# A gated recurrence and a mixer on one core: part of the transposes moved from TensorE to the DMA crossbar

## The chip, the cores and the metric

The kernel runs on one core of one Trainium2 chip. The metric is the device time of one launch in microseconds. PE is TensorE, DVE is VectorE, ACT is ScalarE, POOL is GpSimd, and SP is the sync engine, which here issues most of the DMAs.

## The reference

Two parts follow each other. The first is linear attention with a decaying state, for 4 batches, 8 heads, 768 steps and 48 channels a head:

```python
state = alpha[:, :, t, :, None] * state + np.einsum('bhd,bhe->bhde', k[:, :, t], v[:, :, t])
y[:, :, t] = np.einsum('bhd,bhde->bhe', q[:, :, t], state)
```

The second is a mixer on x, which is y with its heads side by side (4 x 768 x 384):

```python
xt = x.transpose(0, 2, 1)
h = np.maximum(xt @ w_tok1, 0.0) @ w_tok2        # 768 -> 256 -> 768, over the steps
u = x + h.transpose(0, 2, 1)
h2 = np.maximum(u @ w_ch1, 0.0) @ w_ch2          # 384 -> 1536 -> 384, over the channels
return u + h2
```

Inputs and output are float32; the kernel multiplies in bfloat16.

## The kernel before, in words

**Attention.** The 768 steps of a batch are six chunks of 128, numbered 0 to 23 over the four batches. For chunks 6 to 23 (`attention`, one chunk at a time) ACT takes the logarithm of alpha (line 412), PE sums it over the steps with a triangular matrix (lines 418 and 421), and ACT takes two exponentials, `a` and `ia` (lines 426 and 428). POOL makes `pkk`, k times `ia` (line 434); POOL or DVE makes `pkq`, q times `a` (line 438). Both have the steps on the partitions. The scores need them with the channels there, so PE transposes them in eight blocks into one bank of PSUM (line 454, operations `trk` and `trq`), and ACT or DVE copies the bank to SBUF as `tp` (line 458). Sixteen small matmuls make the scores (line 469), DVE masks them (line 472), and PE adds the scores times v (line 507) and q times the state before (line 511) to the chunk's output, which is copied out as `x` (line 515). The state goes on from chunk to chunk without the transposed tiles (lines 483, 492 and 498). Batch 0 has a version for pairs of chunks (`attention_pair`).

**Mixer.** For each batch PE runs the two token layers (lines 766 and 788), DVE adds x to give `u` (line 798, six tiles of 128 steps), PE transposes u in two halves of nine blocks (line 834, `utp`; the first half of batch 0 is made in another way), and ACT or DVE copies them as `ut` (line 840). The first channel layer (line 853, 72 matmuls a batch) is followed by a rectifier on ACT or DVE (lines 860 and 861), the second channel layer (line 875) by an addition of u on DVE (line 881), and the output leaves through SP (line 884).

**Loads.** k, q, v and alpha of batches 1 to 3 are loaded by SP, one chunk of one tensor at a time (192 KB in rows of 192 bytes, line 733), into a few buffers each; those of batch 0 in pairs of chunks (line 744); the weights and batch 0's v by POOL.

**What sets the order.** A planner in Python runs at build time: every operation has a cost, its inputs and a rank (`RANKS`, a list of names; the lowest rank goes first), and `schedule` runs them through a model of engines, buffers and DMA queue. The instructions are then written out in the order that the model gave, so each engine, SP's queue too, has a fixed order, and it waits where an input is late. In the model a DMA from SP starts 1.0 us after its issue or when the one before it is through, takes its given time, and has landed 1.2 us later:

```python
t = max(issue + 1.0, self.hw_end)
...
self.hw_end = t + left
return t + left + 1.2
```

`LOADS` ranks the loads of batch 0, `NOT_BEFORE` holds some DMAs back, and warm-up matmuls without a use fill the gaps on PE up to about 36 us (line 377).

Of the kernel before, what the change touches and what calls it, by code (L numbers as in the profile page):

```python
# [9 lines left out]
BF16 = mybir.dt.bfloat16  # L10
# [34 lines left out]
utp3_1_1 ch1_3_0_10 rt1_0_7 ch1_0_0_5 gt4 ch2_0_5_1 y17 ss14 ch1_2_0_5 rt2_1_3 trq20 u1_1 ch2_3_2_1 trq12 ea21
tok1_1_0_5 tok2_0_4 ea23 tk5 vb23 ch1_2_1_11 ch1_3_0_7 u3_0 u3_2 ch2_3_1_1 u0_2 ss12 ei8 kk3 st12 mask5 ht2_1 aq11
kk17 trk18 aq5 mask14 ln15 tp9 ht0_0 ch2_2_2_1 sa20 ln7 gt22 ch1_3_1_9 tok2_1_0 tok1_1_1_3 ln12 o2_2 rt3_0_11 tk0
ss1b ei9 st16 rt0_1_5 u2_5 u0_1 y2 o3_5b qq4 rt3_0_6 ch2_2_3_1 o2_1 ei18 trk4 aq0 trk21 ut0_0_1 ss2 tp7 ln19 ln5 y1
cum7 cum2 y0 gt16 ea4 tok1_0_1_5 y21 vb12 ln2 ea19 o3_4 ea8 rt1_0_5 ch1_3_0_6 ch1_0_0_0 ei5 ch1_2_0_10 st15 rt0_0_3
rt2_1_7 aq7 vb19 out3_0 rt3_0_2 ut1_1_1 sa7 ut3_1_0 rt3_1_5 out2_4 ei7 tok2_3_4 mask10 ei13 tt0_1 trk9 ei2 ln21  # L50
ch2_2_2_2 mask7 trq23 utp1_0_0 ch1_1_1_10 rt0_1_10 ei23 ea11 ch1_3_1_7 ch1_1_1_5 o3_3 lvz2 cum15 out3_2 rt1_1_10
ch1_0_1_7 sa22 st21 out1_5 trk8 ss7 ch2_3_2_0 ch1_0_0_1 kk6 qq5 tp18 x7 ss3 gt15 cum8 tp16 trq22 kk0 aq23 ss1 qq23
ln4 wwt1 u1_0 st18 st20 x10 utp0_1_0 qq14 ch2_1_2_0 ch1_3_0_0 out0_3 rt0_1_7 aq10 rt3_1_2 rt2_1_1 o3_5a trk23 ln18
x3 ut2_1_1 rt0_1_3 out3_3 trk20 gt0 st3 st7 rt3_1_9 st1 rt2_1_2 tp6 tok2_0_3 ch1_0_0_2 ut2_1_0 trk16 wwc20 rt1_1_4
ea10 rt3_0_9 ch1_0_0_3 st4 y9 tok2_0_5 rt1_1_11 wwc10 y16 trq3 ch1_0_0_11 utp0_1_1 rt3_0_1 ln1 ss6 ch1_3_1_6
ch1_3_1_2 ea3 ch1_0_0_9 rt0_1_0 trq19 trq8 ch1_1_1_0 tok1_3_0_0 u3_3 x17 aq15 tok2_0_2 qq10 x1 qq21 tok2_3_0 out3_1
ch2_1_0_2 lvz5 trq13 aq16 ch1_0_1_4 tok2_0_1 ch1_0_1_1 ch1_0_1_11 aq12 rt1_0_1 cum11 ch1_0_1_6 trq11 out1_4 tok2_3_1
tok1_3_0_3 ch1_0_0_7 ch1_2_0_7 ch1_0_1_3 o2_3 ut0_0_0 vb22 tok2_1_1 tok2_0_0 mask15 ea12 trq21 st14 u2_0 gt3
ch2_0_2_1 tok2_1_3 wwc21 ch1_0_1_5 aq3 u0_4 rt0_0_11 st22 ch1_0_1_0 vb16 trk7 tp23 wwc22 mask8 ss3b rt0_0_8 trq5
qq19 rt2_1_10 ch1_0_1_9 mask21 ss5 rt0_1_4 ei1 tok1_1_0_0 ln22 tok2_2_1 ch2_3_4_2 rt3_0_10 tk1 tok1_1_1_5 ln9 st19  # L60
out0_4 utp1_0_1 y7 ch1_0_1_10 rt0_0_6 ch2_3_5a_1 kk15 x15 kk8 rt3_0_4 ch1_0_1_8 ch2_0_0_0 aq18 utp2_0_1 rt1_0_11
out3_4 out1_1 ch2_2_4_0 ch2_3_0_0 y11 ch2_0_5_0 ea15 ch1_3_1_5 vb13 o0_4 tq3 u2_1 rt3_1_4 aq1 ch1_3_1_1 rt2_1_6
tok1_3_1_0 qq20 ch2_0_1_0 ss4 ch2_2_0_2 ch2_0_3_0 tok2_1_5 tp10 ss22 trq0 ch1_1_1_9 ch1_3_0_8 mask4 y23 u0_0
ch1_3_0_5 rt0_0_9 tok1_0_1_3 o1_2 vb21 mask6 rt0_1_9 tok1_0_0_5 ch1_2_1_2 rt2_1_0 tok2_1_4 rt3_0_8 st5 lvz0 mask3
utp3_0_1 rt1_0_9 cum22 aq8 kk13 ch2_2_1_1 ss21 ch2_3_1_0 rt1_0_2 trq10 out1_3 ln3 kk19 gt14 rt3_0_3 rt2_0_3 tok2_2_2
ch2_3_1_2 mask13 ch1_2_1_1 ut2_0_1 ch1_1_1_7 kk22 ch1_2_0_4 ln8 tq1 tok1_3_1_5 o2_4 aq17 o3_1 ch2_2_5_2 ht1_1 ei12
aq20 y22 ss15 y18 ln14 ch1_2_1_7 kk5 ch1_1_1_2 ss10 gt11 rt1_0_6 st3b ch1_2_0_2 ch2_1_3_2 st13 rt0_1_6 ss16
ch2_0_3_2 y12 rt1_1_2 out0_5 ch1_1_0_10 tq5 cum0 u2_2 tok1_2_0_5 vb20 out3_5b x22 tok2_2_0 rt2_1_5 ht1_0 ch2_3_0_1
vb6 out0_0 cum20 ch1_1_0_5 vb7 gt17 x4 rt3_1_0 ei4 rt2_0_5 o2_5 gt10 utp2_1_0 ch1_1_1_6 aq13 ei20 cum6 ch1_3_1_0
rt0_0_4 ch2_1_1_1 trk22 o0_0 ch2_3_4_1 ea7 wwc12 ch1_1_1_8 ch1_1_0_1 rt0_0_0 trk14 ei21 ln20 ch2_0_1_2 cum18 u1_2  # L70
ch1_2_1_8 ch1_2_0_3 ch1_1_0_2 ss19 ch2_1_1_0 rt2_0_7 rt3_1_6 out1_2 o3_0 out2_5 ch2_2_1_2 ch1_2_1_3 tok2_2_4 u2_3
ch1_3_0_3 qq0 tq0 rt0_1_1 cum19 rt1_0_0 ei17 ch2_3_5b_2 u0_3 x2 ln11 ch1_2_1_10 o0_5 x12 wwc11 trq18 ht3_1 rt0_0_10
qq9 rt2_0_11 ch2_3_2_2 ch1_1_0_0 vb14 ch1_1_0_3 o2_0 tok1_2_1_3 y5 st8 ei10 ss2b tp21 qq15 rt2_0_9 aq6 trk11 y15
ei22 tok1_2_1_5 aq14 ch1_2_0_8 rt0_0_2 utp2_1_1 sa14 ch2_1_2_2 trq14 ch1_3_1_3 ch1_1_0_9 x19 tok1_2_0_0 rt3_1_8 kk11
rt0_1_2 mask18 trk15 utp1_1_0 vb8 tp22 o0_1 kk1 u0_5 mask9 trk0 ch1_1_0_6 rt3_1_7 ch1_3_1_8 ch1_1_0_11 ch1_2_0_1
ch1_2_0_0 ch2_2_0_1 qq16 ss18 rt2_1_8 u3_5 ch1_3_0_1 out2_2 ut1_0_0 ea0 x13 cum14 sa21 aq2 ea9 rt0_0_7 ea5 st0
ch1_2_1_5 sa16 ch2_3_5a_2 ch2_1_5_2 st1b ch1_1_0_4 kk7 y19 out2_1 mask22 ch2_1_3_0 ln6 tp14 x14 st2b tok2_2_5 cum13
ln16 o1_5 o1_1 trq4 ei15 out3_5a y20 ch2_1_5_0 ch1_3_1_11 ch2_2_3_0 o0_2 ch1_1_0_8 ch2_2_4_1 mask20 ch2_2_5_0 aq4
ea1 ch2_2_0_0 ch2_3_4_0 ch2_1_4_0 x20 trk2 aq22 tp19 ht0_1 trk13 lvz3 ch2_0_4_1 tp12 cum10 tok2_3_2 rt2_0_0 x11 trk5
rt2_0_4 u1_3 ch1_3_0_9 ch2_1_4_2 utp1_1_1 ut3_0_0 ut3_1_1 ch2_2_2_0 y14 trq16 vb10 ln10 gt18 mask1 ch2_1_0_0 qq6  # L80
# [129 lines left out]
def schedule(ops, slots, sw=()):  # L210
# [20 lines left out]
    while ready:  # L231
# [41 lines left out]
        if o.dma:  # L273
            o.done = dmas.land(o.dma[0], t, *o.dma[1:])
# [779 lines left out]
```

## Time and profile before

| | us |
|---|---|
| median of 3 runs | 184.79 |
| lowest and highest run | 184.6 and 186.39 |
| the profiled execution, its own time | 182.94 |
| span of the profiled execution, first to last instruction | 181.2 |
| PE, DVE, ACT, POOL busy in it | 173.9, 105.4, 108.5, 59.7 |

The profile is that of one execution. The busy times are of the whole span and mix stages: loads are on the way up to about 117 us, and only outputs after it. PE busy counts a matmul from its start to a modelled end, so it is read together with the pace of uninterrupted runs. A row of the groups gives the line, the engine, the tiles out and in, the count, the busy time, the mean of one in nanoseconds, and the idle time ahead with what ended it. A row by stretches gives the busy time of PE, weight loads, DVE, ACT and POOL with counts, then the granted clock, the busy share of the DMA engines and what they moved in GB/s.

### The profile page before, as it was taken

How to read it: one execution, taken by the hardware profiler on the slowest of the kernel's cores; microseconds unless marked ns; L12 is line 12 of the kernel's file. 1: busy time of each engine (PE TensorE's matmuls, PEld its weight loads, DVE VectorE, ACT ScalarE, POOL GpSimd, SP SyncE). 2: the span in 40 equal slices, each digit the busy share in tenths (PEclk: the TensorE clock that was granted, in tenths of full speed). 3: DMA queues.
4: the chain of work that ended last, by engine and by line, in shares of the span. 5: the costliest groups of instructions: out<-in, count | busy, mean ns of one | idle time of the engine just before them, and what ended most of it. 6: DMA issues, size and time to landing. Idle time of an engine off the chain costs nothing.

```text
span 181.2 us, 4740 instructions
## 1 busy us (share of the span) xinstructions
PE 173.9 (96%) x1922; PEld 120.7 (67%) x1922; DVE 105.4 (58%) x190; ACT 108.5 (60%) x219; POOL 59.7 (33%) x94
## 2 busy tenths in 40 slices
PE   7897899999999999999899999999999999999994
PEld 4575788677676676677677666577666566676663
DVE  6674676694972665886975579565556652130142
ACT  3456785577894567799787675879732204948000
POOL 8922886020942336456361722403030000000000
PEclk9999999999999999999999999999999999999999
DMA  5999999998999899999999999910002121110123
GB/s 133 201 202 245 225 176 200 194 191 171 203 196 198 159 194 178 201 185 238 205 217 182 228 169 205 259 60 4 0 0 89 45 87 43 47 43 0 43 90 130
DMA packets 93861, 26.45 MB, mean 146 GB/s; under 512 B 88080, under 2 KB 93456, under 8 KB 93840
## 3 DMA queue, kind: packets, MB, share of 16 engines
q1 hardware_dynamic: 87984, 22.42, 59.6%
q0 software_dynamic: 5856, 3.74, 14.2%
q8 instruction: 15, 0.25, 0.6%
q14 instruction: 6, 0.05, 0.1%
HBM read 25.17 MB, written 4.72 MB: 165 GB/s over the span
## 4 chain that ended last, share of the span: by engine, by line
PE 64%; DMA 23%; SPq 4%; ACT 2%; DVE 2%; issue 1%; POOL 1%; DVEq 0%; POOLq 0%; ACTq 0%
PE ps L853 21%; PE ps L875 19%; DMA at_pair<-in_alpha_dram 15%; SPq L744 4%; PE ps L766 3%; PE ps L788 3%; DMA vt_pair<-in_v_dram 3%; PE ps L454 3%; DMA qt_pair<-in_q_dram 3%; DMA at<-in_alpha_dram 3%; PE ps L377 2%; PE p L469 2%; PE ps L834 1%; PE ps L507 1%; PE ps L666 1%
## 5 line engine op out<-in xcount | busy, mean ns | idle before, releaser
L853 PE MATMUL ps<-ut,wc 128*128 128x384 bf16 x288 | 54.3, 326 | 0.9 <-DVE ut L840 0.5
L875 PE MATMUL ps<-wc,rt 128*128 128x384 bf16 (+1 forms) x300 | 52.7, 319 | 0.0
L860 ACT ACTIVATE rt<-ps 128x384 bf16<-128x384 f32 x85 | 41.8, 494 | 12.9 <-PE ps L853 12.4
L853 PEld LDWEIGHTS <-wc 128*128 128x128 bf16 x288 | 30.7, 114 | 13.3 <-issue 1.7
L875 PEld LDWEIGHTS <-rt 128*128 128x128 bf16 x300 | 27.8, 98 | 15.5
L881 DVE TENSOR_TENSOR o<-ps,u 128x384 f32<-128x384 f32 (+1 forms) x25 | 13.3, 540 | 21.6 <-PE ps L875 21.2
L472 DVE TENSOR_TENSOR gtm<-p,u 128x1024 bf16<-128x1024 f32 x18 | 22.0, 1220 | 6.8 <-PE p L469 6.8
L434 POOL TENSOR_TENSOR pkk<-kt_pair,ia 128x384 bf16<-128x384 f32 x15 | 15.3, 1017 | 24.3 <-ACT ia L428 24.2
L798 DVE TENSOR_TENSOR u<-ps,x 128x384 bf16<-128x384 f32 x24 | 12.7, 550 | 6.7 <-PE ps L788 6.7
L458 ACT COPY tp<-ps 128x1024 bf16<-128x1024 bf16 x13 | 13.2, 1014 | 3.3 <-PE ps L454 3.3
L377 PE MATMUL ps<-warm_in 128*128 128x256 bf16 x70 | 13.9, 290 | 0.0
L445 POOL TENSOR_TENSOR acq<-a,bm 128x8 f32<-128x8 f32 x18 | 5.7, 317 | 24.0 <-ACT a L426 22.5
L412 ACT ACTIVATE la<-at_pair 128x384 bf16<-128x384 f32 x15 | 7.9, 528 | 8.7 <-DMA at_pair<-in_alpha_dram 8.6
L788 PE MATMUL ps<-ht,wt 128*128 128x384 bf16 x48 | 11.0, 326 | 0.0
L438 DVE TENSOR_TENSOR pkq<-qt_pair,a 128x384 bf16<-128x384 f32 x9 | 7.1, 784 | 6.1 <-DMA qt_pair<-in_q_dram 4.4
L492 DVE TENSOR_TENSOR sum<-ps,ss 128x384 f32<-128x384 f32 x12 | 6.6, 552 | 6.2 <-PE ps L483 6.2
L766 PE MATMUL ps<-x,wt 128*128 128x384 bf16 x48 | 9.9, 326 | 0.0
L428 ACT ACTIVATE ia<-ps 128x384 f32<-128x384 f32 x18 | 8.9, 492 | 1.3 <-PE ps L421 1.3
L840 ACT COPY ut<-ps 128x384 bf16<-128x384 bf16 (+1 forms) x7 | 4.2, 611 | 9.0 <-PE ps L834 9.0
L426 ACT ACTIVATE a<-ps 128x388 f32<-128x388 f32 x18 | 8.8, 491 | 0.6 <-PE ps L421 0.5
L515 ACT CAST x<-ps 128x384 bf16<-128x384 f32 x12 | 5.8, 481 | 5.1 <-PE ps L511 5.0
L611 DVE TENSOR_TENSOR gtm<-p,mask_pair 128x1024 bf16<-128x1024 f32 x6 | 7.3, 1223 | 2.0 <-PE p L606 1.8
(118 smaller groups left out, 267.1 us busy)
## 6 DMA issues: line engine op xcount, KB each, us to landing
out_dram<-o SPq DMA_DIRECT2D x23, 192.0 KB, 3.0
at_pair<-in_alpha_dram SPq DMA_DIRECT2D x21, 192.0 KB, 4.5
kt_pair<-in_k_dram SPq DMA_DIRECT2D x21, 192.0 KB, 4.7
qt_pair<-in_q_dram SPq DMA_DIRECT2D x21, 192.0 KB, 4.8
vt_pair<-in_v_dram SPq DMA_DIRECT2D x14, 192.0 KB, 4.4
wc<-in_moe_w_ch_dram POOLq DMA_DIRECT2D x6, 384.0 KB, 9.1
vt<-in_v_dram SPq DMA_DIRECT2D x4, 192.0 KB, 4.0
wt<-in_moe_w_tok_dram POOLq DMA_DIRECT2D x2, 384.0 KB, 7.1
```

The lines of the kernel that those rows point to most:

```text
L377: last = g.op("PE", f"warm_{i}", lambda e, ps=ps: e.matmul(ps()[:, 0:256], lhsT=E.warm_in[:, 0:128], rhs=E.warm_in, start=True, stop=True, ...
L428: g.op("ACT", f"ei{n}", lambda e: e.activation(ia(), cum()[:, 0:HD], AF.Exp, scale=-1.0), act_us(384), reads=[cum], writes=[ia])
L434: g.op("POOL", f"kk{n}", lambda e: e.tensor_tensor(pkk()[:, :, 0:D], T["kt"](), hd(ia()), ALU.mult), (1.03, 1.0), reads=[T["kt"], ia], wri ...
L458: lambda e: (e.copy if e is E.act else e.tensor_copy)(tp(), ptp().bitcast(BF16).rearrange("p (j t) -> p j t", t=128)),
L472: g.op("DVE", f"mask{n}", lambda e: e.tensor_tensor(gtm(), E.p23.rearrange("p (j t) -> p j t", t=128), E.mask8, ALU.mult), (1.24, 1.22), r ...
L766: e.matmul(ps()[:, 0:HD], lhsT=E.b_wt1[:, kc, m * 128:m * 128 + 128], rhs=x[kc](), start=(kc == 0), stop=(kc == NS - 1), skip_group_check= ...
L788: e.matmul(ps()[:, 0:HD], lhsT=E.b_wt2[:, kc, i * 128:i * 128 + 128], rhs=ht[kc](), start=(kc == 0 and not summed), stop=(kc == NDT - 1))
L798: g.op("DVE", f"u{b}_{i}", lambda e, ps=ps, t=t, i=i: e.tensor_tensor(t(), ps()[:, 0:HD], x[i](), ALU.add), dve_us(384), reads=[ps, xt[i]] ...
L853: e.matmul(ps()[:, 0:384], lhsT=E.by_four[mc // 4][:, kc, mc % 4, :], rhs=uts[half]()[:, kc * 384:kc * 384 + 384], start=(kc == 0), stop=( ...
L860: e.activation(rtt[mc]()[:, cs], ps()[:, 0:384], AF.Relu) if e is E.act else
L875: e.matmul(ps()[:, 0:n], lhsT=rtt[mc]()[:, i * 128:i * 128 + 128], rhs=E.b_wc2[:, mc, cs], start=(mc == 0), stop=(mc == NDC - 1), skip_gro ...
L881: g.op("DVE", f"o{tag}", lambda e, ps=ps, t=t, i=i, cs=cs, n=n: e.tensor_tensor(t()[:, cs], ps()[:, 0:n], u[i]()[:, cs], ALU.add), dve_us( ...
```

## The change

For chunks 12 to 23 (batches 2 and 3) k and q are written into one tile `pk` of 128 x 1024, and SP issues one transposing DMA from SBUF to SBUF that writes `tp`. The eight transposes on PE and the copy out of PSUM are gone for these chunks. For batches 1, 2 and 3 three tiles of u lie in one tile `u3` of 128 x 1152, and one transposing DMA a half writes `ut`; nine transposes on PE and two copies are gone for each. These are 12 + 6 = 18 transposing DMAs, all issued by SP, in its written order among loads and outputs. Since the blocks of `ut` lie in another order, the first channel layer reads it in three runs of 128 columns.

The planner's model changes with it. SP's next instruction now waits until at most 2,048 rows are on the way (`gate`; a load counts 1,024, a transposing DMA 128). A transposing DMA holds SP for 1.3 us (1.35 for u) and the queue for 0.9 us (1.0). Some other DMA costs are changed. `RANKS`, `LOADS`, `NOT_BEFORE` and two parameters are new, so the order of all instructions is a new one from the start on. The loads of batch 0's second and third pair are one DMA instead of two. Buffers: `u` 13 to 6 with 4 of `u3`, `rt` 24 to 18 with the six halves of batch 0's v reused after it, `pkk` 6 to 4 with 3 of `pk`, `tp` 3 to 4, `acq` 6 to 5, `o` 7 to 6.

```diff
+    CROSS_KQ, CROSS_U = tuple(range(12, 24)), (1, 2, 3)
...
+    def gate(self):
+        runs = 0
+        for end, count in reversed(self.flying):
+            runs += count
+            if runs > 2048:
+                return end
+        return 0.0
...
+            if e == "SP":
+                free[e] = max(free[e], dmas.gate())
...
+        crossbar = n in self.CROSS_KQ
+        if crossbar:
+            tk = tq = g.tile(self.s_pk)
+            pkk, pkq = (lambda: tk()[:, 1]), (lambda: tk()[:, 0])
+        else:
+            tk, tq = pkk, pkq = g.tile(self.s_pkk), g.tile(self.s_pkq)
...
+        if crossbar:
+            g.op("SP", f"dtk{n}", lambda e: e.dma_start_transpose(
+                tp(), tk().rearrange("p w h d -> p (w h d)")), (1.3, 1.3), reads=[tk], writes=[tp],
+                dma=("hw", 0.9, 1.0, 128))
+        else:
             g.op("PE", f"trk{n}", ...
             g.op("PE", f"trq{n}", ...
             g.op(("DVE", "ACT"), f"tp{n}", ...
...
+            if b in self.CROSS_U:
+                g.op("SP", f"dtu{b}_{half}", lambda e, t=t, h=ut3[3 * half]: e.dma_start_transpose(
+                    t().rearrange("p (j t) -> p j t", t=128), h()), (1.35, 1.35), reads=[ut3[3 * half]],
+                    writes=[t], dma=("hw", 1.0, 1.0, 128))
+                uts.append(t)
+                continue
...
+            if b in self.CROSS_U:
+                return t.rearrange("p (i j t) -> p j i t", i=3, j=3)[:, kc]
...
-                                 rhs=uts[half]()[:, kc * 384:kc * 384 + 384], start=(kc == 0),
+                                 rhs=channels(uts[half](), kc), start=(kc == 0),
...
-            (0.66, 0.66), writes=[t], follow=self.last, at=n - 999.0, dma=("hw", 0.955))
+            (0.66, 0.66), writes=[t], follow=self.last, at=n - 999.0 if n < 12 else 66.0 + 4.2 * (n - 12), dma=("hw", 0.955, 1.0, 1024))
...
+        split = ci // 2 in self.SPLIT
+        for grp in range(2) if split else (None,):
...
+        for t in bufs(E.s_pk, [128, 2, H, 64], BF16):
+            dve.memset(t[:, :, :, D:64], 0.0)
```

More of the change, by code (lines that the diff above doesn't have):

```diff
@@ L76 @@
[L76 to L80, printed above, removed]
@@ L182, in __init__, with land @@
         self.sw_made = []
-    def land(self, kind, issue, need, part=1.0):
+        self.flying = []
+    def gate(self):
[5 more added lines that the diff above has]
+        return 0.0
+    def land(self, kind, issue, need, part=1.0, runs=0):
         if kind == "sw":
-            s = max(issue + 2.0, self.sw_end)
+            s = max(issue + 2.2, self.sw_end)
             self.sw_end = s + need
@@ L206, in land @@
         self.hw_end = t + left
+        self.flying.append((t + left, runs))
         return t + left + 1.2
@@ L675, in attention_pair @@
         self.y[n] = g.op("PE", f"y{n}", f_y, (c, c + DRAIN),
-                         reads=[gtm, vz, tq] + [t for t in before if t], writes=[py],
+                         reads=[gtm, tq] + vz + [t for t in before if t], writes=[py],
                          follow=self.y.get(n - 1))
```

225 lines of the change are left out of this document (124 added, 101 removed), and 2 rows, old and new, of the table PLAN.

## The prediction

> **What bounds the kernel now.** I read the parts of the page first, then the busy time by stretches, then the chain that ended last.
>
> ```profile
> span 181.2 us, 4740 instructions
> PE 173.9 (96%) x1922; PEld 120.7 (67%) x1922; DVE 105.4 (58%) x190; ACT 108.5 (60%) x219; POOL 59.7 (33%) x94
> DMA  5999999998999899999999999910002121110123
> ...
> 15.00:20.00 5.00, 3.28 (x37) 2.29 (x35) 2.40 (x5) 2.76 (x7) 2.97 (x5) 1.00 1.05 256
> 50.00:55.00 5.00, 5.00 (x67) 3.52 (x66) 3.72 (x6) 5.00 (x12) 2.59 (x5) 1.00 1.06 202
> 105.00:110.00 5.00, 5.00 (x59) 3.35 (x58) 4.66 (x9) 3.89 (x6) 1.31 (x3) 1.00 0.93 170
> 120.00:125.00 5.00, 5.00 (x75) 3.69 (x74) 3.86 (x6) 4.45 (x11) 1.39 (x2) 1.00 0.04 14
> ```
>
> Two resources are full at once for most of the span. The DMA row is at 8 or 9 through slice 26 (to 118 us) and nearly idle after it; PE is full from about 50 us to the end. In the stretches the last columns are granted clock, DMA share and GB/s: at 105 to 110 us both PE and DMA are full, at 120 to 125 us PE alone. The clock is 1.00, so no step below needs a slower one.
>
> A busy PE need not be a PE at its pace, so I took the pace from the chain, where uninterrupted runs stand:
>
> ```profile
> 41.21 0.45 PE ps L454 x8
> 158.59 0.50 PE ps L834 x9
> 160.40 5.85 PE ps L853 x36
> 166.25 11.73 PE ps L875 x84
> ```
>
> A 384-column matmul takes 5.85/36 = 0.1625 us, and the eight transposes of k and q of one chunk 0.45 us. The last 84 matmuls run back to back. The queue side:
>
> ```profile
> 59.89 0.52 ACT L412 ACTIVATE la<-at_pair 128x384 bf16<-128x384 f32 x1 [2.57 <-DMA at_pair<-in_alpha_dram]
> 103.32 0.52 ACT L412 ACTIVATE la<-at_pair 128x384 bf16<-128x384 f32 x1 [0.97 <-DMA at_pair<-in_alpha_dram]
> 112.53 0.94 SPq L733 DMA_DIRECT2D vt_pair<-in_v_dram  x1
> 113.52 65.22 SPq L884 DMA_DIRECT2D out_dram<-o  x20
> ```
>
> ACT still waits for alpha at 60 and at 103 us: until the last load is issued at 112.53 us, attention goes at the pace of the loads, and PE stays busy only because the mixer of an earlier batch fills in. How much of that filling is left is what decides this change:
>
> ```profile
> L511 PE MATMUL ps<-ss,tp 128*128 128x96 bf16 x40 | 3.3, 204 | 0.0
> 98.19 0.33 PE L511 MATMUL ps<-ss,tp 128*128 128x96 bf16 x4
> 80.00:100.00 20.00, 0.00 (x0) 0.00 (x0) 1.00 1.10 212
> 100.00:115.00 15.00, 7.40 (x41) 3.80 (x42) 1.00 1.08 199
> 101.37 2.62 PE ps L875 x16
> ```
>
> The first row groups 50 to 115 us: ten runs of four state matmuls, five for each batch, and the second row is the last of the ten. It belongs to chunk 17, the last of batch 2: its output is there at about 99 us, and the mixer of batch 2 can begin. The two rows by stretch are line 875 alone: none ran from 80 to 100 us, so all 72 second-layer matmuls of batch 1 were still to come, 72 x 0.1625 = 11.7 us of work. That is the cover: if batch 2 arrived up to 11.7 us later, PE would still have had work.
>
> **The change part by part.** *Removed from PE:* 12 chunks x 0.45 = 5.4 us, and six halves of u x 0.50 = 3.0 us. Together 8.4 us on an engine that is full from 50 us on, and a full PE gives back what is taken from it as long as its next work has arrived.
>
> *Removed from ACT and DVE:* the twelve evictions of k and q and the twelve of u.
>
> ```profile
> L458 ACT COPY tp<-ps 128x1024 bf16<-128x1024 bf16 x13 | 13.2, 1014 | 3.3 <-PE ps L454 3.3
> L840 ACT COPY ut<-ps 128x384 bf16<-128x384 bf16 (+1 forms) x7 | 4.2, 611 | 9.0 <-PE ps L834 9.0
> ```
>
> I price them at nothing: ACT at 60% and DVE at 58% have room, and the work that hides them is PE's. Were PE starved instead, they would stand in its place, about a microsecond for a chunk.
>
> *Added to the queue:* 18 transfers of 256 or 288 KB through SP. No transposing transfer stands in the trace, so I bound its queue time by rows of the loads.
>
> ```profile
> DMA packets 52891, 10.95 MB, mean 199 GB/s; under 512 B 52243, under 2 KB 52883, under 8 KB 52883
> GB/s 133 201 202 245 225 176 200 194 191 171 203 196 198 159 194 178 201 185 238 205 217 182 228 169 205 259 60 4 0 0 89 45 87 43 47 43 0 43 90 130
> at_pair<-in_alpha_dram SPq DMA_DIRECT2D x10, 192.0 KB, 4.2
> out_dram<-o SPq DMA_DIRECT2D x23, 192.0 KB, 3.0
> ```
>
> The first and third rows are of the stretch from 60 to 115 us: 52,891 packets over 16 engines in 55 us are 16.6 ns a packet. If a k and q transfer is read in rows of 256 bytes it has 1,024 of them, 64 an engine, so 1.06 us; by bytes at the best slice, 259 GB/s, it is 1.01 us. That is the low end. The high end is a transfer that overlaps with nothing, as long as an output from issue to landing, 3.0 us. Loads are issued about a microsecond apart and land 4.2 us after issue, so several overlap; I take 1.5 us, near the low end, which leaves 0.4 us for SP to get the queue full again behind each.
>
> The Trainium skill, page DMA: Bandwidth & Descriptors, section Latency and other measured facts, gives 261 GB/s for a transposing DMA with a non-contiguous middle dimension; an estimate from it is 1.0 us for 256 KB, and the sum below would then end near -7.4 us instead of -3.5. No run here shows a transpose yet.
>
> *What is late next.* Before chunk 17 is done, eight transfers go through the full queue: k and q of chunks 12 to 17 and the two halves of u of batch 1. They push the loads behind them back by 8 x 1.5 = 12.0 us. Chunk 17 itself now also waits for a landing, 3.0 us by the row of the outputs, where PE and one copy stood. So batch 2 arrives 15.0 us later. The cover is 11.7 us, less the work that PE no longer has by then, 6 x 0.45 + 2 x 0.50 = 3.7 us: 8.0 us. To it come chunks 18 and 19, which need nothing of batch 2's mixer:
>
> ```profile
> 45.83 0.35 PE p L469 x16
> ...
> 49.95 0.36 PE L507 MATMUL ps<-vb,gtm 128*128 128x48 bf16 x8
> 50.31 0.65 PE L853 MATMUL ps<-ut,wc 128*128 128x384 bf16 x3
> 52.09 0.33 PE L418 MATMUL ps<-la,u 128*128 128x384 bf16 x1
> 52.35 0.33 PE L483 MATMUL ps<-vb,pkk 128*128 128x96 bf16 x4
> 52.52 0.39 PE L454 MATMUL ps<-id,pkk 128*128 128x128 bf16 x4
> ```
>
> By the starts, scores take 0.35, the output 0.36, the running sum 0.26 and the state 0.17 us: 1.14 us a chunk, 2.1 us for these two, the first of which has no state part. PE therefore idles 15.0 - 8.0 - 2.1 = 4.9 us. With 1.06 us a transfer it is 8.5 + 3.0 - 10.1 = 1.4 us; with 3.0 us it is 24.0 + 3.0 - 10.1 = 16.9 us; a gain beyond the 8.4 us is excluded, since no other PE work leaves.
>
> *Batch 3.* Its transfers meet an emptying queue (share 0.04 at 120 us), and second-layer matmuls of batch 2 hide the landing of its u:
>
> ```profile
> 145.00:160.00 15.00, 8.48 (x47) 4.40 (x47) 1.00 0.15 54
> ```
>
> Of line 875, 47 matmuls (7.6 us) run between the last token layer and the last run of line 853, against two landings of 3.0 us. Without that cover these would cost 6.0 us.
>
> *SP's waits.* Each transfer waits on SP for k and q to be ready, with all later loads and outputs behind it, and after 113 us also behind outputs that wait for VectorE:
>
> ```profile
> SPq L884 <- DVE o L881: 55.9, 16, 17.4
> ```
>
> In the written order an output that waits 17.4 us stands ahead of nothing that others need; in the new order a k and q transfer can stand behind it. I price this at nothing because the loads in flight, 4.2 us of them, feed the queue through a wait of one or two microseconds; longer waits are the slower rival below.
>
> *The rest.* Larger loads for pairs 1 and 2, weights asked for at other times, other buffer counts and the new order before 60 us act where the queue is full anyway and PE has 1.7 us of idle (row 15 to 20 us). I take 0, bounds -1.7 and +1.7 us.
>
> Sum: -8.4 + 4.9 + 0 = **-3.5 us**. The profiled execution has a span of 181.2 us, and its own time is 182.94 us, 1.74 us around the span. It would go to 179.4 us. The median of the three runs, 184.79 us, lies 1.85 us above that execution, so the forecast for the median is **181.3 us**, with a range of its own from 177.8 (1.06 us a transfer) to 182.9.
>
> **The rivals.** *All is hidden* (176.4 us): transfers at the low end, and landings that the order has foreseen. For it: chunk 23 has its alpha logarithm at 113 us and its running sum only at 132 us, so batch 3 can come later. Against it: the alpha waits at 60 and 103 us.
>
> *Slower: the fixed order cannot use the cover.* PE takes its instructions in the written order, so a transposed tile that lands later than the planner thought stops PE on the spot, whatever other work exists. The planner gives a k and q transfer 1.0 + 0.9 + 1.2 = 3.1 us from issue. An output of 192 KB takes 3.0 us; scaled by bytes to 256 KB that is 4.0 us, so 0.9 us too late each time. Twelve for k and q are 10.8 us and the two of batch 3's u 1.8 us, 12.6 in all, for the four others have the second layer of the batch before in between. Result 12.6 - 8.4 = +4.2 us, 189.0 us. It turns slower where a landing is over 8.4/14 = 0.6 us late. For it: PE's order is static and SP's too. Against it: under the present order PE idled only 0.8 us ahead of line 853 in the 65 us of full queue.
>
> ```profile
> 113.04 0.52 ACT L412 ACTIVATE la<-at_pair 128x384 bf16<-128x384 f32 x1 [1.17 <-DMA at_pair<-in_alpha_dram]
> 132.27 0.33 PE L418 MATMUL ps<-la,u 128*128 128x384 bf16 x1
> L853 PE MATMUL ps<-ut,wc 128*128 128x384 bf16 x94 | 18.8, 327 | 0.8 <-DVE ut L840 0.5 <-ACT ut L840 0.2
> ```
>
> *The load stream decides the end, and nothing is won.* All but the transfers of batch 3's u, 16 x 1.5 = 24 us, push the last load's landing from 112.5 + 4.2 = 116.7 to 140.7 us. Chunk 17 took about 6 us from landing to output (its last load, six chunks of four ahead of the last one, went out at 87.72 us), so with 3 us for the crossbar the last output is at 149.7. Behind it stand the twelve matmuls of the second token layer, 1.95, u's landing, 3.0, both channel layers, 23.4, and the last output, 3.2 (the span's end less 178): 181.25 us of span, so 184.8 us. For it: ACT's waits for alpha. Against it: the order now leaves 38 us between the last attention and the end, and these need 31.6.
>
> ```profile
> 87.72 0.72 SPq L733 DMA_DIRECT2D vt_pair<-in_v_dram  x1
> 140.03 0.33 PE L511 MATMUL ps<-ss,tp 128*128 128x96 bf16 x4
> ```
>
> *Block by block.* If the crossbar takes each block of 128 by 128 as a transfer of its own, a k and q transfer is eight slots of 1.06 us, 8.5 us; sixteen of them add 136 us to the queue, about 24 of them hidden: near 297 us. The Trainium skill, VectorE: DVE Perf Modes, section The three transpose paths, speaks for it and against this change: 1309 ns for such a block by DMA and 390 ns on TensorE. The trace shows the second to be lower when eight run in a row (0.45 us for eight); it has nothing on the first.
>
> **How the numbers follow.** Forecast 0.38, all hidden 0.07, load stream 0.13, late landings 0.37, block by block 0.05. Faster by over 1% (about what a measurement of this kernel can tell from no change) is the first two, 0.45; the load stream is within 1%, 0.13; slower the last two, 0.42. Forecast and late landings are nearly even, for both follow from transfers that come late, and they differ only in whether PE has other work in its written place; the recorded idle of 0.8 us tips it. The range goes from 176.6 to 193.3 us, the latter +8.5 us, which is 16.9 us of idle at 3.0 us a transfer; late landings lie inside.
>
> **What would show it right or wrong.** Right: 48 matmul transposes left on line 454's successor and 9 on that of 834; PE busy with under 165 us; one gap of about 5 us on PE at 100 to 115 us, ended by work of batch 2; the last load issued 8 to 20 us after 112.5; a transpose 1 to 2 us apart from the next issue on SP. Wrong: many gaps of about a microsecond ahead of the score matmuls (late landings), SP waiting long for k or q while the DMA row drops below 9 before 110 us, landings of transposes over 5 us with an idle queue, or PE without gaps but the end not earlier.

## The result, and the profile after

The changed kernel is slower: 190.71 us median of 4 runs (189.97 to 190.87), against 185.59 us for the kernel before on the same chip. The ratio is 1.034, 95% interval 1.028 to 1.040. Medians here hold all runs of a kernel, and ratios only those within 1.5% of its fastest, so that the two do not always divide out. The forecast was 181.3 us; the result lies between the rival of the late landings, 189.0 us, and the upper end of the range, 193.3 us. The profiled execution took 190.83 us with a span of 189.1, which is 7.9 us more than the 181.2 before.

First the page after: span, busy times, DMA in 40 slices.

```profile
span 189.1 us, 4430 instructions
PE 166.9 (88%) x1772; PEld 112.0 (59%) x1772; DVE 96.5 (51%) x176; ACT 98.3 (52%) x210; POOL 58.1 (31%) x94
DMA  5999999989997979999999999999998025140024
```

PE has 7.0 us less to do (166.9 against 173.9), and it idles 22.2 us where it idled 7.3: 14.9 us more idle, less 7.0 us of work, is the 7.9 us. After its first slice the DMA row stays at 7 to 9 through slice 31, 147 us; before, it fell after slice 26, at 118 us.

Where the idle time stands is in the busy time by stretches (PE, weight loads, DVE, ACT, POOL, then clock, DMA share and GB/s). The kernel before:

```profile
0.00:70.00 70.00, 65.93 (x815) 47.28 (x816) 45.77 (x95) 44.68 (x91) 33.47 (x57) 1.00 1.06 191
70.00:100.00 30.00, 29.32 (x392) 20.84 (x391) 22.38 (x34) 24.70 (x52) 15.52 (x23) 1.00 1.09 204
70.00:140.00 70.00, 69.09 (x840) 47.69 (x839) 47.68 (x73) 50.64 (x102) 26.25 (x38) 1.00 0.77 152
```

After:

```profile
0.00:70.00 70.00, 62.35 (x795) 44.77 (x795) 42.37 (x91) 44.57 (x92) 35.24 (x59) 1.00 1.08 190
70.00:100.00 30.00, 23.05 (x275) 14.93 (x274) 17.77 (x30) 14.33 (x33) 8.96 (x14) 1.00 1.21 185
70.00:140.00 70.00, 58.46 (x613) 37.22 (x612) 38.85 (x61) 35.27 (x81) 22.34 (x34) 1.00 1.14 192
140.00:189.00 49.00, 46.12 (x368) 30.04 (x365) 15.28 (x26) 18.50 (x39) 0.50 (x1) 1.00 0.34 95
```

From 70 to 140 us PE idles 11.5 us instead of 0.9: 10.6 of the 14.9 us, 6.3 of them by 100 us already (7.0 us of idle time instead of 0.7). Another 3.6 us lie ahead of 70 us (7.7 instead of 4.1), before any transposing transfer had landed. From 140 us on PE is nearly full again, with work that is late. The clock is 1.00 in these rows, so it has no part in this.

The lateness comes from SP's queue. SP's timeline after (start, duration; SPq is the issuing itself), from the last load that both kernels issue at the same time (65.57 us; 65.60 before) to the last load of all:

```profile
65.57 2.70 SPq L765 DMA_DIRECT2D kt<-in_k_dram  x1
...
69.91 1.91 SPq L483 DMA_TRANSPOSE tp<-pk  x1
...
97.74 0.53 SPq L765 DMA_DIRECT2D vt_pair<-in_v_dram  x1
...
131.96 3.41 SPq L870 DMA_TRANSPOSE ut<-u  x1
...
138.14 0.58 SPq L765 DMA_DIRECT2D vt_pair<-in_v_dram  x1
...
155.00 1.30 SPq L870 DMA_TRANSPOSE ut<-u  x1
```

The loads are level when the first transposing transfer goes out at 69.91 us. Seven transfers later chunk 17's last load is issued at 97.74, 10.0 us later than before (87.72); fourteen transfers later the last load of all at 138.14, 25.6 us later than before (112.53). The loads fall behind step by step: chunk 13's last load is 2.7 us late, chunk 17's 10.0, chunk 23's 25.6. A transfer holds SP for 1.3 us when the queue has room (155.00) and for up to 3.4 us when it is full (131.96).

Who waits for it: in the view of the waits, ACT for alpha before,

```profile
ACT la L412 <- DMA at_pair<-in_alpha_dram: 8.6, 7, 2.6
```

and after (total, times, longest), with the transfers' row, SP's duration of one as minimum, median and maximum in ns, and their landings:

```profile
ACT la L432 <- DMA at_pair<-in_alpha_dram: 22.2, 13, 6.0
PEld L501 <- DMA tp<-pk: 6.3, 8, 2.2
PE p L501 <- DMA tp<-pk: 4.0, 3, 1.9
PE ps L906 <- DMA ut<-u: 3.9, 3, 1.5
SPq L483 <- POOL acq L472: 4.7, 3, 2.3
L483 SPq DMA_TRANSPOSE tp<-pk x12: 1275/1864/3123, 69.9 to 142.1; - x12
DMA to landing us min/median/max: 3.1/4.0/5.6
```

ACT waits for alpha 22.2 us instead of 8.6. PE itself stops for `tp` (4.0 us; its weight loads, which run beside it, 6.3) and for `ut` (3.9 us). Four of these stops, shown further down, are 5.9 of the 7.0 us that PE idles from 70 to 100 us. This view alone leaves open whether the transfers are late by themselves, or because of the full queue in which they stand together with the loads.

### The profile page after: what moved, and what is told of

It is laid out like the page before. It is cut to its first block, busy times and chain, and to the rows that moved or that the text cites. A ratio compares the mean times of both kernels' runs of the same rounds, so it can differ in the third digit from the quotient of the medians.

```text
span 189.1 us, 4430 instructions
## 1 busy us (share of the span) xinstructions
PE 166.9 (88%) x1772; PEld 112.0 (59%) x1772; DVE 96.5 (51%) x176; ACT 98.3 (52%) x210; POOL 58.1 (31%) x94
## 3 DMA queue, kind: packets, MB, share of 16 engines
q0 software_dynamic: 5856, 3.74, 13.4%
## 4 chain that ended last, share of the span: by engine, by line
PE 40%; DMA 34%; SPq 16%; ACT 4%; issue 2%; DVE 2%; POOL 1%; POOLq 0%; DVEq 0%
DMA at_pair<-in_alpha_dram 15%; PE ps L928 13%; PE ps L906 12%; SPq L765 7%; DMA tp<-pk 5%; DMA vt_pair<-in_v_dram 5%; SPq L777 3%; DMA ut<-u 3%; SPq L870 3%; SPq L483 2%; DMA out_dram<-o 2%; PE ps L397 2%; PE ps L800 2%; DMA kt_pair<-in_k_dram 2%; PE ps L829 2%
## 5 line engine op out<-in xcount | busy, mean ns | idle before, releaser
L928 PE MATMUL ps<-wc,rt 128*128 128x384 bf16 (+1 forms) x222 | 46.1, 322 | 0.0
L913 ACT ACTIVATE rt<-ps 128x384 bf16<-128x384 f32 x62 | 29.6, 492 | 17.1 <-PE ps L906 16.8
L928 PEld LDWEIGHTS <-rt 128*128 128x128 bf16 x222 | 20.9, 98 | 12.1
L934 DVE TENSOR_TENSOR o<-ps,u 128x384 f32<-128x384 f32 (+1 forms) x25 | 13.4, 540 | 26.1 <-PE ps L928 23.7
L432 ACT ACTIVATE la<-at_pair 128x384 bf16<-128x384 f32 x15 | 7.8, 522 | 22.2 <-DMA at_pair<-in_alpha_dram 22.2
L928 PE MATMUL ps<-wc,vz 128*128 128x384 bf16 (+1 forms) x78 | 19.2, 314 | 0.0
L839 DVE TENSOR_TENSOR u<-ps,x 128x384 bf16<-128x384 f32 x24 | 12.9, 553 | 11.5 <-PE ps L829 11.4
L461 POOL TENSOR_TENSOR pk<-kt_pair,ia 128x384 bf16<-128x384 f32 x10 | 10.8, 1081 | 11.7 <-DMA kt_pair<-in_k_dram 6.0
L397 PE MATMUL ps<-warm_in 128*128 128x256 bf16 x70 | 13.4, 275 | 0.0
L913 ACT ACTIVATE vz<-ps 128x384 bf16<-128x384 f32 x22 | 10.5, 488 | 3.6 <-PE ps L906 3.6
L501 PE MATMUL p<-tp 48*64 48x128 bf16 x288 | 7.5, 222 | 4.3 <-DMA tp<-pk 4.0
L465 DVE TENSOR_TENSOR pk<-qt_pair,a 128x384 bf16<-128x384 f32 x9 | 6.4, 720 | 9.5 <-DMA qt_pair<-in_q_dram 9.4
L530 POOL TENSOR_TENSOR ss<-sum,acq 128x384 bf16<-128x384 f32 x9 | 8.1, 901 | 9.4 <-DVE sum L524 9.4
L800 PE MATMUL ps<-x,wt 128*128 128x384 bf16 x48 | 10.8, 326 | 0.1
L467 POOL CAST vb<-vt_pair 128x384 bf16<-128x384 f32 x9 | 4.5, 504 | 19.3 <-DMA vt_pair<-in_v_dram 15.1
```

The source lines that it names most:

```text
L397: last = g.op("PE", f"warm_{i}", lambda e, ps=ps: e.matmul(ps()[:, 0:256], lhsT=E.warm_in[:, 0:128], rhs=E.warm_in, start=True, stop=True, ...
L461: g.op("POOL", f"kk{n}", lambda e: e.tensor_tensor(pkk()[:, :, 0:D], T["kt"](), hd(ia()), ALU.mult), (1.03, 1.0), reads=[T["kt"], ia], wri ...
L800: e.matmul(ps()[:, 0:HD], lhsT=E.b_wt1[:, kc, m * 128:m * 128 + 128], rhs=x[kc](), start=(kc == 0), stop=(kc == NS - 1), skip_group_check= ...
L839: g.op("DVE", f"u{b}_{i}", lambda e, ps=ps, uv=uv, i=i: e.tensor_tensor(uv(), ps()[:, 0:HD], x[i](), ALU.add), dve_us(384), reads=[ps, xt[ ...
L913: e.activation(rtt[mc]()[:, cs], ps()[:, 0:384], AF.Relu) if e is E.act else
L928: e.matmul(ps()[:, 0:n], lhsT=rtt[mc]()[:, i * 128:i * 128 + 128], rhs=E.b_wc2[:, mc, cs], start=(mc == 0), stop=(mc == NDC - 1), skip_gro ...
```

## The experiments

All eleven are below, in the order in which they ran. Ratios are to the kernel before, timed on the same chip; the last column is the issue of the last load, chunk 23's v.

| kernel | median us | ratio [95%] | span us | last load us |
|---|---|---|---|---|
| before | 185.59 | | 181.2 | 112.53 |
| after | 190.71 | 1.034 [1.028, 1.040] | 189.1 | 138.14 |
| e1_tiny | 177.12 | 0.968 [0.958, 0.979] | 175.7 | 121.46 |
| e2_copy | 186.83 | 1.021 [1.011, 1.032] | 186.1 | 132.69 |
| e3_half_after | 178.86 | 0.970 [0.958, 0.981] | 175.7 | 122.27 |
| e4_half_before | 181.50 | 0.990 [0.985, 0.996] | 181.2 | 99.62 |
| e5_dummy | 200.49 | 1.102 [1.087, 1.117] | 197.9 | 131.20 |
| e6_first_tiny | 180.74 | 0.989 [0.976, 1.003] | 178.2 | 126.11 |
| e7_last_tiny | 185.36 | 1.009 [1.003, 1.016] | 180.8 | 126.56 |
| e8_late_u3 | 182.08 | 0.993 [0.990, 0.997] | 180.6 | 118.43 |
| e9_late_u23 | 181.79 | 0.991 [0.986, 0.996] | 179.9 | 124.56 |
| e10_four_u23 | 184.43 | 1.002 [0.996, 1.007] | 184.4 | 116.34 |
| e11_replanned | 189.50 | 1.029 [1.019, 1.039] | 187.4 | 134.74 |

### The same order, with transfers of almost no bytes

```diff
-            g.op("SP", f"dtk{n}", lambda e: e.dma_start_transpose(
-                tp(), tk().rearrange("p w h d -> p (w h d)")), ...
+            g.op("SP", f"dtk{n}", lambda e: e.dma_start(
+                tp()[:, 0, 0:16], tk()[:, 0, 0, 0:16]), ...
# and for u: t()[:, 0:16] from h()[:, 0:16]
```

> The changed kernel in its own order, but each of the 18 crossbar transfers is a plain DMA of 4 KB from the same source to the same destination (the transposed tiles are not made). Load stream (each crossbar transfer takes about 1.75 us from the stream of loads, the last load leaves 25 us late, and everything behind follows): the last load is issued near 114 to 118 us and the time falls to 178 to 183 us. Order (the new order of instructions is poor whatever the transfers cost): the time stays above 187 us.

Measured: 0.968, 177.12 us, span 175.7 us, 13.4 us less than after; the time is a little under the range expected for the load stream and the last load, at 121.46 us, a little later. SP's timeline and busy times by stretch:

```profile
70.31 0.53 SPq L765 DMA_DIRECT2D vt_pair<-in_v_dram  x1
...
121.46 1.51 SPq L765 DMA_DIRECT2D vt_pair<-in_v_dram  x1
0.00:70.00 70.00, 63.08 (x796) 45.41 (x797) 44.43 (x95) 45.25 (x93) 34.99 (x59) 0.98 1.09 191
70.00:140.00 70.00, 69.27 (x766) 45.66 (x767) 45.39 (x70) 41.51 (x94) 24.11 (x35) 1.00 0.76 156
```

With the same order, the same waits on the transfers and the same work removed from PE, PE idles 0.7 us between 70 and 140 us instead of 11.5. So 13.4 us are the price of what the transfers move, their own late landings included; the order alone is not what makes the change slower. Between chunk 13's v and chunk 23's v stand 40 loads and 13 transfers; they take 51.15 us here and 66.27 in the changed kernel (71.87 to 138.14): 1.16 us more for each transfer.

The span is 5.5 us below that of before, not 8.4: the new order, with 18 tiny transfers in it, costs 2.9 us. A loss of that size stands ahead of 70 us: PE idles 6.9 us there instead of 4.1. Less work is done by then, as the second channel layer in the groups up to 70 us shows, before and then here:

```profile
L875 PE MATMUL ps<-wc,rt 128*128 128x384 bf16 x52 | 9.7, 325 | 0.0
```

```profile
L928 PE MATMUL ps<-wc,rt 128*128 128x384 bf16 x36 | 6.8, 326 | 0.1
```

16 fewer of them had run, 16 x 0.1625 = 2.6 us.

### Plain copies of the same size in place of the transposes

```diff
-            ... e.dma_start_transpose(tp(), tk()...)
+            ... e.dma_start(tp()[:, :, 0:126], tk()...[:, :, 0:126])
# 252 of 256 bytes of each block, so that the pieces stay apart; the same for u
```

> The changed kernel in its own order, but each crossbar transfer is a plain DMA of nearly the same bytes in pieces of 252 bytes (1,024 or 1,152 pieces) from the same source to the same destination (nothing is transposed). If bytes and pieces are what costs: 188 to 191 us, last load at 134 to 140 us. If the crossbar or the way in which SP issues it is what costs: the copies take about a microsecond of the stream each, the last load leaves near 126 us, and the time is 181 to 185 us.

Measured: 1.021, 186.83 us, span 186.1 us, last load at 132.69 us, between the two expectations. Two rows of it, SP's timeline and PE's waits:

```profile
70.56 0.68 SPq L483 DMA_DIRECT2D tp<-pk  x1
PE ps L908 <- DMA ut<-u: 4.9, 3, 1.9
```

Between the same two loads 61.39 us pass (71.30 to 132.69), 0.79 us per transfer over the tiny ones against 1.16 for the crossbar. About two thirds of the price are bytes and pieces that a plain DMA of this shape costs too. The rest, 66.27 - 61.39 = 4.9 us over the stretch, is the crossbar's own; for k and q a plain copy holds SP 0.69 us (median), the crossbar 1.86. The two ratios, 1.021 and 1.034, have intervals that overlap, so in the end time this share is indicated and not settled.

### Room in the queue

Loads of k, q and v from chunk 12 on bring only four of the eight heads, in the changed kernel (e3) and in the kernel before (e4).

```diff
+        hn = 4 if n >= 12 and name != "at" else 8
-                t(), getattr(E, E.SRC[name])[b, :, ts:ts + 128, :].transpose([1, 0, 2])),
+                t()[:, 0:hn], getattr(E, E.SRC[name])[b, 0:hn, ts:ts + 128, :].transpose([1, 0, 2])),
```

> The changed kernel with its crossbar transfers, but the loads of k, q and v of chunks 12 to 23 bring only four of the eight heads (the other half of these tiles is left as it was), so that the queue has room. Load stream: 178 to 183 us, PE waits for tp and ut below 4 us in all. Late landings (a crossbar transfer lands later after its issue than the planner figures, 4.0 us against 3.1, and the fixed order of PE stops for each): still above 187 us, with the same waits for tp and ut, about 16 us on PE and its weight loads.

> The kernel before with the same halved loads of k, q and v of chunks 12 to 23; it tells what the halving does without the change. Both theories: PE bounds it after 50 us, so 182 to 185 us, at most 3 us below the kernel before.

Measured: 0.970 and 0.990. With half the load bytes the change makes the kernel about 2% faster (0.970 against 0.990, the intervals lie apart), where with all of them it makes it 3.4% slower. All 18 crossbar transfers are real in e3. SP's timeline, DMA issues (count, us to landing), PE's waits and PE by stretch of e3:

```profile
84.15 1.24 SPq L483 DMA_TRANSPOSE tp<-pk  x1
122.27 1.18 SPq L766 DMA_DIRECT2D vt_pair<-in_v_dram  x1
tp<-pk SPq DMA_TRANSPOSE x12, 3.4
PE ps L907 <- DMA ut<-u: 0.9, 1, 0.9
70.00:140.00 70.00, 68.73 (x753) 45.27 (x751) 45.64 (x69) 40.92 (x93) 23.97 (x35) 1.00 0.88 166
```

A landing takes 3.4 us and PE hardly waits for one. With room in the queue, then, the 18 crossbar transfers cost less than they save; it is in a queue that is already full that they cost the time. These two runs don't tell whether PE loses it to the transfers, which land late in a full queue, or to the loads behind them: with room in the queue both are early.

### Transfers alone, in the old order

The kernel before, whole, with 13 crossbar transfers of the same size into tiles that nobody reads any more, issued behind the loads of k of chunks 13 to 23 and of q of chunks 16 and 20. PE's work and everyone's order are those of before.

```diff
+            if (name, n) in E.EXTRA:
+                ...
+                e.dma_start_transpose(flat[i].rearrange("p (j t) -> p j t", t=128), flat[2])
```

> The kernel before in its own order, with all its work on PE; behind the loads of k of chunks 13 to 23 and of q of chunks 16 and 20 SP issues one more crossbar transfer of 256 KB, 13 in all, between tiles that nobody reads any more. Both theories: 1.2 to 1.8 us of the load stream each, last load issued at 128 to 136 us instead of 112.5. Fixed order (PE stops at each late input and cannot draw on the other batch's matmuls): 195 to 203 us, PE idle 10 us or more. Cover (PE fills the wait with the second channel layer of batch 1, as the prediction reckoned, 11.7 us of it): 185 to 190 us.

Measured: 1.102. SP's last load, PE by stretch and ACT's largest wait:

```profile
131.20 0.54 SPq L733 DMA_DIRECT2D vt_pair<-in_v_dram  x1
70.00:140.00 70.00, 57.58 (x668) 37.91 (x667) 36.84 (x59) 40.59 (x84) 23.02 (x35) 0.95 1.08 195
ACT la L412 <- DMA at_pair<-in_alpha_dram: 25.9, 11, 4.4
```

The last load goes out 18.7 us later (1.44 us for each transfer), and the span is 16.7 us longer. This is the test of the cover that the prediction relied on. The order is the one in which it was counted, 72 second-layer matmuls still to come, and nothing waits for a transfer. Yet PE idles 12.4 us between 70 and 140 us, 6.1 of them by 100 us, when chunk 17's last load was 9.3 us late; of 18.7 us of lateness at the last load only 2.0 are absorbed. So late loads alone are enough to make the kernel slower, without a single wait for a landing. Some of the loss goes with the clock, granted at 0.95 in this stretch: PE's busy time grew by 2.9 us over the span (176.8), its idle time by 13.8. With the 2.9 set apart, at most 4.9 of 18.7 us are absorbed, about a third of the cover, which is 11.7 + 2.1 = 13.8 us where nothing is taken from PE.

### Which transfers cost most

First the eight ahead of chunk 18 tiny and ten real (e6), then the other way round (e7).

```diff
+                tp()[:, 0, 0:16], tk()[:, 0, 0, 0:16]) if n < 18 else e.dma_start_transpose(
# u: tiny if b == 1; in e7: tiny if n >= 18, and for u if b > 1
```

> The changed kernel in its own order; the eight transfers ahead of the mixer of batch 2 (k and q of chunks 12 to 17, u of batch 1) are plain DMAs of 4 KB (these transposed tiles are not made), the ten others are crossbar transfers. Load stream with a fixed order: each half of the transfers costs in proportion to the number ahead of the last load, so about half of the 14 us between all and none comes back: 182 to 185 us. Cover: the eight ahead of batch 2 are hidden by it, and taking them away gives under 3 us: 188 to 190 us.

> The counterpart: the eight first transfers are crossbar transfers, the ten later ones (k and q of chunks 18 to 23, u of batches 2 and 3) are plain DMAs of 4 KB (these transposed tiles are not made). Load stream with a fixed order: the other half comes back, 182 to 185 us. If only what is on its way before batch 2's mixer hurts PE: 187 to 190 us, for the later ones meet an emptier queue.

Measured: 0.989 and 1.009. Against the 1.034 of the change, taking the eight early transfers away gives back 4.5% of the time before, taking the ten late ones away 2.5%, and taking all away (0.968) 6.6%: within the intervals the parts add up. The first is more than either theory expected. PE's idle time from 70 to 140 us is 3.2 and 3.5 us in these two against 11.5 with all. The early ones push every load of batches 2 and 3, the late ones fewer. That the eight cost more than the ten is indicated and not settled: the two intervals touch at 1.003, and e7 had a clock of 0.94 from 70 to 100 us.

### Fewer transfers, planned with the measured price

k and q by crossbar only for chunks 18 to 23 and u for batch 3 (e8) or batches 2 and 3 (e9), or chunks 20 to 23 and u of batches 2 and 3 (e10). The planner is told that a transfer holds the queue for 1.9 us (k and q) and 2.1 us (u), and the order is planned anew.

```diff
-    CROSS_KQ, CROSS_U = tuple(range(12, 24)), (1, 2, 3)
+    CROSS_KQ, CROSS_U = (18, 19, 20, 21, 22, 23), (2, 3)
-                dma=("hw", 0.9, 1.0, 128))
+                dma=("hw", 1.9, 1.0, 128))
# this is e9; u: 1.0 -> 2.1; new RANKS and WAIT; buffers: u 12, u3 3, pk 2
```

> A new version: crossbar transfers only for k and q of chunks 18 to 23 and u of batch 3 (8 transfers); batch 2 and u of batches 1 and 2 go back to PE. The planner's price of a transfer on the queue is 1.9 us (2.1 for u) instead of 0.9 (1.0), and the order is planned anew with it. Only about six of the transfers lie ahead of the last load, so it leaves 8 to 12 us later than before, at 120 to 125 us. Load stream with a fixed order: the order now knows the price, so PE no longer stops at tp; 6 x 0.45 + 2 x 0.50 = 3.7 us of PE work are gone: 179 to 183 us. If the crossbar costs more than it saves at any place: 185 to 190 us.

> The same with u of batch 2 also by the crossbar (10 transfers, 4.7 us of PE work gone), order planned anew with 1.9 and 2.1 us. Load stream with a fixed order: 178 to 183 us. If the crossbar costs more than it saves at any place: 185 to 190 us, and above the version with 8 transfers.

> The same with k and q of chunks 20 to 23 only and u of batches 2 and 3 (8 transfers, 3.8 us of PE work gone), order planned anew with 1.9 and 2.1 us; two fewer transfers lie ahead of the last load. Load stream with a fixed order: 178 to 183 us, last load 2 to 4 us earlier than in the version with 10. If the crossbar costs more than it saves at any place: 185 to 190 us.

Measured: 0.993, 0.991 and 1.002. e9 has ten transfers and beats both kernels: 0.9% faster than before, interval 0.4 to 1.4%. Its page, PE by stretch, and the largest wait of PE or its weight loads for a transfer:

```profile
PE 169.2 (94%) x1838; PEld 117.3 (65%) x1838; DVE 102.7 (57%) x182; ACT 102.2 (57%) x214; POOL 60.4 (34%) x93
70.00:140.00 70.00, 68.83 (x815) 46.30 (x814) 46.42 (x69) 47.32 (x102) 23.91 (x34) 1.00 0.91 176
PEld L974 <- DMA ut<-u: 0.7, 1, 0.7
```

PE gave up 4.7 us of work and idles 1.2 us between 70 and 140 us. Five of its ten transfers stand ahead of the last load, which is 12.0 us later than before. e10 has two transfers fewer and a last load that is only 3.8 us later, and brings nothing; 178 to 183 us were expected. Each of the three has an order of its own, so the differences among them are also those of the orders. No run has a newly planned order without transfers, so how much of e9's 0.9% comes from the transposes is not shown.

### All 18, planned with the measured price

```diff
-                dma=("hw", 0.9, 1.0, 128))
+                dma=("hw", 1.9, 1.0, 128))
# u: 1.0 -> 2.1; new RANKS and WAIT; which transfers are made is unchanged
```

> All 18 crossbar transfers of the changed kernel, but the planner reckons 1.9 us of queue for a transfer of k and q and 2.1 us for one of u instead of 0.9 and 1.0, and the order is planned anew. If the loss came from a wrong price in the plan (a fixed order that meets late inputs): PE waits for tp and ut fall below 3 us and the time to 182 to 186 us. If it is the stream itself (transfers between loads make batches 2 and 3 late whatever the order): the waits for tp and ut fall, PE idles elsewhere, ahead of work that hangs on loads, and the time stays at 187 to 192 us.

Measured: 1.029 [1.019, 1.039], as slow as the change itself. SP's last load, PE's largest wait in attention and PE by stretch:

```profile
134.74 0.53 SPq L833 DMA_DIRECT2D vt_pair<-in_v_dram  x1
PE ps L607 <- DVE gtm L572: 3.6, 2, 3.2
80.00:90.00 10.00, 5.91 (x92) 3.75 (x90) 8.49 (x14) 3.81 (x9) 3.25 (x5) 0.76 1.16 195
```

The waits of PE for `tp` and `ut` are gone from the list: an order that knows the price avoids the stops on late tiles. The last load is still 22.2 us later than before, and PE idles instead between other steps of attention (4.1 us in this stretch). Over the span PE idles 15.8 us: 6.4 less than in the changed kernel, 8.5 more than before. That the time hardly falls is also due to the clock, 0.76 in this stretch and 0.83 from 70 to 100 us: PE is busy for 171.6 us, 4.7 more than in the changed kernel with the same work. So the wrong price in the plan seems to have a part in the loss, but an order that knows the price still idles more than the kernel before. What this order would cost at full clock, and whether a better one exists, is open.

## Why the prediction was wrong

**What bounds the kernel.** Borne out. DMA and PE were both full from 50 to 118 us, and both resources decided: taking load bytes away turned the change into a gain (e3 against e4), and adding transfers alone made the old kernel 10% slower (e5).

**Removed from PE.** 8.4 us forecast, 7.0 measured in busy time, in which matmuls that start alone count longer than those back to back (12 of line 928 took 2.28 us from 80 to 90 us, 0.19 each, against 0.1625 at their pace). With tiny transfers busy time was 165.0, 8.9 us less. The term was right, though the sign named for it, busy time under 165, was set too low.

**The price of a transfer.** 1.5 us forecast. Measured 1.43 us for each of the seven ahead of chunk 17's last load (10.0/7, on the low side, since three outputs stood among these loads before and none after) and 1.44 in the old order (18.7/13), 1.83 over all fourteen ahead of the last load (25.6/14, with two more outputs and the new order in it), and 1.16 over a tiny transfer in the same place. The term was right too. An estimate from the 261 GB/s of the Trainium skill (DMA: Bandwidth & Descriptors, Latency and other measured facts) is 1.0 us; the traces don't agree: all the measured prices are above it, the lowest by 16%.

**Chunk 17.** Forecast 15.0 us late, with eight transfers and a landing ahead of it. It was 10.2 us late: its outputs, line 543 now, are the last row here of PE's timeline after; the rows above it are four of PE's stops.

```profile
79.80 0.42 PE L501 MATMUL p<-tp 48*64 48x128 bf16 x16 [1.85 <-DMA tp<-pk]
85.30 0.42 PE L501 MATMUL p<-tp 48*64 48x128 bf16 x16 [1.50 <-DMA tp<-pk]
87.32 0.65 PE L906 MATMUL ps<-ut,wc 128*128 128x384 bf16 x3 [1.06 <-DMA ut<-u]
98.17 1.14 PE L906 MATMUL ps<-ut,wc 128*128 128x384 bf16 x6 [1.49 <-DMA ut<-u]
108.36 0.33 PE L543 MATMUL ps<-ss,tp 128*128 128x96 bf16 x4
```

By the working of the prediction 10.2 us against a cover of 10.1 (8.0 + 2.1) would have cost next to nothing.

**The step that failed: "PE therefore idles 15.0 - 8.0 - 2.1 = 4.9 us".** It was 14.9 us more idle in all. The cover was not there when it was needed. Line 928, the second channel layer, in the changed kernel by stretch (PE and weight loads alone):

```profile
70.00:80.00 10.00, 4.56 (x24) 2.20 (x24) 1.00 1.20 175
80.00:90.00 10.00, 2.28 (x12) 1.12 (x12) 1.00 1.24 196
90.00:100.00 10.00, 0.00 (x0) 0.00 (x0) 1.00 1.19 183
100.00:110.00 10.00, 0.98 (x6) 0.53 (x6) 1.00 1.10 200
110.00:120.00 10.00, 6.26 (x37) 3.35 (x36) 1.00 1.06 203
120.00:130.00 10.00, 5.77 (x33) 2.84 (x31) 1.00 1.00 215
```

The 36 before 90 us finish batch 0 (with 36 ahead of 70 us), so all 72 of batch 1 were still to come at 100 us, when PE had already idled 7.0 us. They need the first channel layer of batch 1, which itself waited for `ut`. Its groups from 70 to 101 us, before and after:

```profile
L853 PE MATMUL ps<-ut,wc 128*128 128x384 bf16 x72 | 14.1, 327 | 0.5 <-DVE ut L840 0.5
L906 PE MATMUL ps<-ut,wc 128*128 128x384 bf16 x48 | 8.9, 326 | 3.2 <-DMA ut<-u 2.6 <-ACT vz L913 0.7
```

All 72 of them were done by 101 us before, and 48 after. The 2.1 us of chunks 18 and 19 were no cover either: their loads stand behind the same transfers (the last ones 10.8 and 13.9 us late). The prediction treated lateness as one event, at the end of batch 2, and set the whole stock of later work against it. In fact the lateness grows over all chunks from 13 (2.7 us) to 23 (25.6 us), and PE, which takes its instructions in the written order, stops on the way: from 60 to 140 us 4.0 us at the scores of line 501, 3.9 at the first channel layer, 2.7 at the running sums behind a late alpha. The rows at 79.80, 85.30, 87.32 and 98.17 us above are 5.9 of the 7.0 us up to 100 us, each ended by a transfer. e5 shows the same without any of these waits: there the late loads alone cost 12.4 us of idle time, and 2.0 to 4.9 of 18.7 us were absorbed.

**The sum, term by term.** Forecast -8.4 + 4.9 + 0 = -3.5. By e1, which splits it: -8.4, then +2.9 for the new order with the tiny transfers in it ("the rest", bounds -1.7 to +1.7, exceeded by 1.2), then +13.4 for the transfers: +7.9. The term that failed is the 4.9. (A price of 1.0 us gives -7.5 by the same working; the prediction has -7.4.)

**Batch 3, SP's waits, evictions.** The prediction let all transfers of batch 3 meet an emptying queue. Only the last ones did: the DMA row was full to 147 us, and k and q of chunks 18 to 21 and both halves of u of batch 2 went out ahead of the last load at 138.14. The transfers of batch 3's u, the first at 155.00 us with 1.3 us on SP, did meet an empty queue; the three waits of matmuls for `ut` were at 87, 98 and 137 us, all earlier. SP's waits ahead of transfers were of one or two microseconds, as supposed (2.3 us the longest), and the DMA engines stayed busy through them. The price of the evictions, nothing, was not tested by itself; ACT has 10.2 us less to do.

**The rivals.** *The fixed order cannot use the cover* was the right mechanism for the changed kernel, and its 189.0 us is the nearest number. It made the landings responsible, 0.9 us late each time and 12.6 us in all. Landings of 4.0 us in the median are its number, and PE's stops for `tp` and `ut`, 7.9 us, are most of the 11.5 us from 70 to 140 us; 3.9 of them are for `ut` of batches 1 and 2, which it had taken for covered. Two things it lacked. The transfers are so late only in a full queue: in e3 they land in 3.4 us and PE waits 0.9 us for `ut`. And the loads behind them are late too, which costs time even where nothing waits for a landing (e5). e11, without these stops, has 6.4 us less idle time and is nearly as slow, in part by its clock; so how the 13.4 us of the transfers divide between late landings and late loads is open. *The load stream decides the end* had the stream right: it put the last load 24 us later (25.6 measured) and the last attention output at 149.7 us (148.2 measured). It failed in what follows: it had 31.6 us of work behind that, and there were 40.9, for batch 2's second layer was not done in the meantime. *All hidden* is near what e1 shows for transfers without bytes. *Block by block* is out: eight blocks land in 3.1 to 5.6 us, so the 1309 ns a block that the Trainium skill gives (VectorE: DVE Perf Modes, The three transpose paths) doesn't multiply when eight go in one transfer. The advice of the same page of the Trainium skill (Rules for kernel authors), TensorE for a transpose of 128 by 128 where the result may go to PSUM, held for the change as a whole; what the runs show as the reason is the full queue.

**The signs.** Of the signs of being wrong, the gaps of about a microsecond ahead of the scores appeared (1.85 and 1.50 us above). The one gap of 5 us at 100 to 115 us did not, and the last load came 25.6 us after 112.5, outside the 8 to 20 that were named as right.

## What to carry to other kernels

When two resources are full in the same stretch, work moved from one to the other costs its whole queue time there, and in a kernel with a written order most of it can reach the end (16.7 of 18.7 us in e5, 2.9 of them with a slower clock). Before counting later work as cover, ask whether it is ready and stands in the order at the place where the first late input stops the engine, and whether its own inputs are late by the same cause; lateness begins with the first item behind the added transfer, not with the last. Moving only the ten latest of the 18, half of them behind the last load and with an order of their own (e9), came out 0.9% faster than before, where all 18 lost 3.4%.

## What the hardware showed that was not expected

A transposing transfer of 256 KB from SBUF to SBUF holds the issuing queue of SP for 1.24 us when there is room (e3), 1.86 us in the median and up to 3.1 us in the full queue (288 KB: up to 3.4), where a plain copy of nearly the same pieces holds it 0.69 us in the median. Its landing takes 3.1 us at best and up to 5.6 us in the full queue. The granted clock fell in several stretches in which PE had idled: 0.76 from 80 to 90 us in e11 (PE busy 5.91 of 10 us) and 0.95 in the mean from 70 to 140 us in e5. In rows of 1 us it is 0.50 there, and 1.00 but for a row at each edge: 0.50 from 86 to 95 us in e11, behind 3.15 us without a matmul, and for some three microseconds from 101 and from 122 us in e5, behind 2.11 and 2.37 us. In e7 it fell at 84 us behind gaps of only 0.70 and 1.07 us, and in the profiled execution of the changed kernel it did not fall behind 1.85 and 1.50 us; what sets it is open.
